# Memory-augmented attention and linear attention interleaved: row transposes moved to DMA, shared weight loads, merged left scores, column tiles throughout, a new instruction order

## The chip, the cores and the metric

The kernel runs on one core of one Trainium2 chip. Its engines run at the same time, each through a queue of its own in a fixed order: PE (TensorE, matmuls; weight loads are a queue of their own beside it, PEld), DVE (VectorE), ACT (ScalarE), POOL (GpSimd) and SP (SyncE); the last two mostly issue DMAs here. Semaphores order work between engines. The metric is the device time of one execution in microseconds. Before the change it is 1606.12 us, the median of 3 runs (1605.98 to 1608.79).

## The reference

A sequence of 2048 rows of 512 numbers (bf16) goes through four blocks with residuals: x = x + A(norm(x)), x = x + B(norm(x)), and both once more with the same weights.

```python
# A: memory-augmented attention, 32 heads of 128, segments of 32 rows, 8 memory rows
mem = mem0
for s in range(n_seg):                       # 64 segments, one after the other
    h = concat([mem, x[:, 32*s:32*s+32]])    # 40 rows
    q, k, v = h@Wq, h@Wk, h@Wv               # 512 -> 32 x 128 each
    p = softmax(mask(q k^T / sqrt(128)))
    o = (p v) @ Wo
    mem = o[:, :8]                           # feeds the next segment
    outs.append(o[:, 8:])
# B: linear attention, 32 heads of 16
q, k, v = split(x @ wqkv)
pq, pk = phi(q), phi(k)                      # phi(t) = (t+1 if t>0 else exp(t)) + 1e-6
kv, z = pk^T v, sum(pk)                      # over all 2048 rows
o = (pq kv / (pq z + 1e-6)) @ wo
```

The 8 memory rows that a segment puts out go into the next segment. So the 128 segments of both A blocks are a recurrence, and the second A block of a row tile can start only when the B block before it has seen all rows.

## The kernel before

The sequence is cut into 16 tiles of 128 rows, four segments to a tile. All weights stay in SBUF. `a_layer` runs the 64 segments of an A block. `layer` 0 is the first pair of blocks, `layer` 1 the second.

A segment's matmuls get 32 of its 40 rows as stationary operand: the 8 memory rows and 24 of the 32 new rows. The other 8 rows of each segment (the *left* or displaced rows) are put together for four segments into one block of 32 rows, which is projected once for each tile (`left_block`, steps left0, left1, leftv). A stationary operand of 32 columns fills a quarter of the array, so four matmuls with the same stationary rows run side by side in four column tiles; below, four such matmuls are a *quad*. `project` (L1140) does this for K, Q (halves b = 0 and 1 of the heads: steps kq0, kq1) and V. For several parts it loads the stationary rows for the first part (L1159) and runs the others again on them (L1055, `again`). `fresh` says for how many matmuls the later part loads anew; for V it is set from `FRESH`.

For each half of the heads, `turned` copies K and Q from PSUM and turns them by a 32x32 block transpose on DVE (L1177). `mem_attention` then makes the scores of the segment (L1260) and of the displaced keys against the memory's queries (L1266), their exponential (L1277), two mask multiplies (L1287), the sums, their reciprocal as exp(-ln) (L1296, L1298), the product with V and the normalisation (L1309): these are the rows that become the next memory. `x_attention` does the same for the other rows, later and off the recurrence. The scores of the displaced queries against the displaced keys are made once for a tile, in the step lefts (L1209) at the end of `left_block`, with their exponential (L1216) and mask (L1218).

`out_proj` multiplies by Wo (64 matmuls of 256 columns, L1402). The result stands as two halves in PSUM partitions 0 to 63 and 64 to 127, which have to be added. Two copies of 128x128 bring it to `outW` as fp32. `next_mem` (L1426) adds the halves, turns the 8 rows with a selection matrix in fp32 on PE, and a copy puts them into the next segment's block. `rows_out` adds the halves once more on DVE (L1437) for the residual, and DMAs on POOL and SP put the rows in place (dx_sb).

`layernorm` (L1093) normalises a tile of rows (L1105) and turns it by 16 transposes on PE (L1113); `prepare` (A) and `b_in` (B) copy the turned tile out of PSUM. `b_in` projects K, V and, transposed, Q, applies `phi`, and adds to the sums kva and za. In layer 0 it uses matmuls on the whole 128x128 array (`whole`, L1051), in layer 1 column tiles (`tiled`, L1067). Q is stored transposed in a DRAM scratch (pq_scratch), the rows in another (xs_scratch). `b_mid` masks the sums and folds wo in. `b_out` loads both again, divides (L1669 to L1672) and adds the product to the rows. In layer 0 it runs within the segments of the next A block; in layer 1 all 16 tiles stand at the end.

The order is written out by hand. Every operation is added under a place (layer, step, name, number), and a table gives each place a number; operations with two possible engines have a letter for ACT or DVE. `schedule` sorts all operations by this number, and each engine's queue runs in that order, so a waiting instruction holds all that stand behind it on its engine. Before the change the table is a period of four segments (`PERIOD`) with exceptions (`OWN`). `spin` adds matmuls without use, at the start and between blocks.

## Time and profile before

| what | value |
|---|---|
| runs, median (lowest to highest) | 1606.12 us (1605.98 to 1608.79) |
| span of the profiled execution, first to last instruction | 1603.9 us |
| PE busy | 1542.4 us, 96% |
| weight loads busy | 881.7 us, 55% |
| DVE busy | 1219.1 us, 76% |
| ACT busy | 1101.0 us, 69% |
| POOL busy | 200.1 us, 12% |
| DMA, mean over the span | 32 GB/s |
| weights land (Wk, Wq, Wv after issue) | 13.8, 24.5, 34.0 us |

The profile shows one execution; its span is the time from the first to the last instruction, and the time of a run lies a little above it. An engine's busy time counts moments in which at least one of its instructions runs. Matmuls overlap, so the busy time of a group of them says nothing of what it adds to the stream; the distance between the start of one and the start of the next does. "Idle before, releaser" names what an engine waited for. The chain goes back from the last instruction to what released it, step by step. A few matmul records are missing from the trace.

### The profile page before, as it was taken

The page shows a single profiled execution, that of the slowest core. Times are in us where ns is not written, and L with a number is a line of the kernel's source. Part 1 is how long each engine was busy: PE and PEld are TensorE (multiplying, and loading weights), DVE is VectorE, ACT ScalarE, POOL GpSimd, SP SyncE. Part 2 cuts the span into 40 slices and gives each one's busy share as a digit, 9 for nine tenths or more (in the row PEclk, how much of TensorE's full clock was granted, in tenths as well). Part 3 has the DMA queues.
Part 4 walks back from the last instruction along what each step waited for, and adds up shares of the span by engine and source line. Part 5 has one row for each costly group of instructions (what it writes and reads, how often), then busy time and mean ns, then how long its engine had stood idle before and what let it go on. Part 6 is the DMA issues. An engine that isn't in the chain of part 4 may idle for free.

```text
span 1603.9 us, 104195 instructions
## 1 busy us (share of the span) xinstructions
PE 1542.4 (96%) x52074; PEld 881.7 (55%) x43287; DVE 1219.1 (76%) x3865; ACT 1101.0 (69%) x3212; POOL 200.1 (12%) x408
## 2 busy tenths in 40 slices
PE   5899999999999999999999999999999999999997
PEld 1455555556555555555545565655655556556564
DVE  3778788877888887887677777777777777777777
ACT  1566666766666677676566777777778777777765
POOL 2011110111111111111101111111110111110110
PEclk9999999999999999999999999999999999999999
DMA  9300000000000000000000000000000000000014
GB/s 380 106 13 14 10 17 16 17 17 14 17 10 18 16 17 17 18 16 16 26 8 14 17 17 20 20 14 17 20 18 19 20 14 17 21 18 18 27 34 141
DMA packets 33567, 50.95 MB, mean 32 GB/s; under 512 B 10600, under 2 KB 27272, under 8 KB 31592
## 3 DMA queue, kind: packets, MB, share of 16 engines
q1 hardware_dynamic: 19288, 26.46, 4.7%
q0 software_dynamic: 13680, 17.69, 3.7%
q8 instruction: 374, 6.13, 1.6%
q14 instruction: 65, 0.53, 0.1%
q10 hardware_dynamic: 160, 0.14, 0.0%
HBM read 29.63 MB, written 10.49 MB: 25 GB/s over the span
## 4 chain that ended last, share of the span: by engine, by line
PE 89%; DVE 4%; ACT 3%; DMA 2%; issue 1%; POOL 0%; DVEq 0%; SPq 0%
PE pb L1159 27%; PE pb L1055 23%; PE pb L1402 18%; PE pb L1067 11%; PE pb L1051 3%; DMA Wv_sb<-in_A_Wv_dram 2%; ACT arena_sb L939 2%; PE pb L1260 1%; PE pb L1426 1%; PE pb L1113 1%; PE pb L1340 1%; DVE st_sb L1099 1%; DVE arena_sb L1287 0%; DVE arena_sb L940 0%; PE pb L1209 0%
## 5 line engine op out<-in xcount | busy, mean ns | idle before, releaser
L939 ACT ACTIVATE arena_sb<-pb 128x512 bf16<-128x512 f32 (+5 forms) x1234 | 556.3, 485 | 276.3 <-PE pb L1055 181.6
L1159 PE MATMUL pb<-Wk_sb,arena_sb 128*32 128x512 bf16 x4096 | 410.7, 380 | 5.5 <-DMA Wq_sb<-in_A_Wq_dram 3.2
L1055 PE MATMUL pb<-Wq_sb,arena_sb 128*32 128x512 bf16 x4096 | 410.2, 379 | 0.0
L940 DVE CAST arena_sb<-pb 128x512 bf16<-128x512 f32 (+3 forms) x510 | 275.6, 544 | 105.7 <-PE pb L1055 66.5
L1402 PE MATMUL pb<-Wo_sb,arena_sb 128*32 128x256 bf16 x10368 | 346.7, 273 | 5.5 <-issue 2.7
L1067 PE MATMUL pb<-arena_sb 128*32 128x128 bf16 (+2 forms) x12528 | 327.2, 216 | 5.2 <-DVE arena_sb L1606 2.0
L1067 PEld LDWEIGHTS pb<-arena_sb 128*32 128x32 bf16 x12528 | 227.7, 96 | 131.0 <-issue 38.8
L1177 DVE STREAM_TRANSPOSE arena_sb<-arena_sb 128x256 f32<-128x256 f32 x640 | 261.4, 431 | 50.1 <-ACT arena_sb L939 43.5
L1159 PE MATMUL pb<-Wv_sb,arena_sb 128*32 128x512 bf16 x3136 | 281.2, 378 | 1.3 <-DMA Wv_sb<-in_A_Wv_dram 0.6
L1402 PEld LDWEIGHTS pb<-Wo_sb,arena_sb 128*32 128x32 bf16 x10368 | 258.8, 96 | 37.2 <-issue 11.3
L1159 PEld LDWEIGHTS pb<-Wk_sb,arena_sb 128*32 128x32 bf16 x4096 | 122.2, 96 | 251.7 <-issue 176.5
L955 POOL DMA_DIRECT2D dx_sb<-y_sb x252 | 128.1, 512 | 1010.7 <-DVE y_sb L1437 496.7
L1055 PE MATMUL pb<-Wv_sb,arena_sb 128*32 128x512 bf16 x1984 | 210.5, 378 | 0.0
L939 ACT ACTIVATE arena_sb<-arena_sb 32x256 bf16<-32x256 bf16 (+1 forms) x377 | 143.2, 380 | 14.5 <-DVE arena_sb L1347 4.6
L1159 PEld LDWEIGHTS pb<-Wv_sb,arena_sb 128*32 128x32 bf16 x3136 | 90.5, 96 | 78.7 <-issue 24.5
L939 ACT ACTIVATE outW_sb<-pb 128x128 fp32r<-128x128 f32 x294 | 67.6, 275 | 77.9 <-PE pb L1402 69.7
L1287 DVE TENSOR_TENSOR arena_sb<-arena_sb 128x128 bf16<-128x128 bf16 x504 | 91.7, 216 | 29.6 <-ACT arena_sb L1277 27.9
L1277 ACT ACTIVATE arena_sb<-pb 128x192 bf16<-128x192 f32 (+1 forms) x256 | 85.0, 333 | 41.6 <-PE pb L1260 38.4
L1309 DVE TENSOR_TENSOR arena_sb<-pb,arena_sb 128x128 bf16<-128x128 f32 x252 | 72.9, 289 | 50.3 <-PE pb L1067 25.2
L1159 PE MATMUL pb<-Wq_sb,arena_sb 128*32 128x512 bf16 x1024 | 103.4, 378 | 0.2
L1055 PE MATMUL pb<-Wk_sb,arena_sb 128*32 128x512 bf16 x1024 | 103.0, 378 | 0.0
L940 DVE COPY arena_sb<-arena_sb 32x256 bf16<-32x256 bf16 (+1 forms) x391 | 80.1, 208 | 9.1
(110 smaller groups left out, 1789.3 us busy)
## 6 DMA issues: line engine op xcount, KB each, us to landing
Wk_sb<-in_A_Wk_dram SPq DMA_DIRECT2D x1, 4096.0 KB, 13.8
Wq_sb<-in_A_Wq_dram SPq DMA_DIRECT2D x1, 4096.0 KB, 24.5
Wv_sb<-in_A_Wv_dram SPq DMA_DIRECT2D x1, 4096.0 KB, 34.0
Wo_sb<-in_A_Wo_dram SPq DMA_DIRECT2D x16, 256.0 KB, 7.3
xs_scratch<-x_sb POOLq DMA_DIRECT2D x32, 128.0 KB, 2.8
pq_scratch<-arena_sb POOLq DMA_DIRECT2D x32, 128.0 KB, 3.1
x_sb<-xs_scratch POOLq DMA_DIRECT2D x16, 128.0 KB, 2.4
arena_sb<-pq_scratch POOLq DMA_DIRECT2D x16, 128.0 KB, 2.4
```

The costliest lines, as they stand in the source:

```text
L939: return e.activation(o() if callable(o) else o, i() if callable(i) else i, ACTF.Copy)
L940: return e.tensor_copy(o() if callable(o) else o, i() if callable(i) else i)
L955: add(eng, lambda e: e.dma_start(o, i), 0.55 if eng == "pool" else 0.4, reads=reads, writes=writes, dsem="%s%d" % (kind, k), lat=lat + (0. ...
L1051: return pe.matmul(o, w, x, start=start, stop=stop, skip_group_check=True)
L1055: return pe.add_instruction(mybir.InstMatmult(name=nc.get_next_instruction_name(), engine=mybir.EngineType.PE, ins=[pe.lower_ap(x), pe.low ...
L1067: r = pe.matmul(o[q], w[:, q], x, start=start, stop=stop, skip_group_check=True, tile_position=(0, 32 * j))
L1159: r = pe.matmul(o, blk[:, c, :], w, start=(c == 0), stop=(c == 3), tile_position=(0, 32 * j))
L1177: add("dve", lambda v: v.transpose(dst, src(img[:, k, :].bitcast(F32))), 0.445, reads=[("img", k)], writes=[dkey])
L1277: add("act", lambda a: a.activation(PQ[:, r2, b, 0:nq], tl.f32()[:, 0:nq], ACTF.Exp, scale=SCALE), c_act(nq), tiles=[tl], writes=[("PQ", r ...
L1287: add("dve", lambda v, a=a, p_=p_, w_=w_: v.tensor_tensor(wide(Pm[:, k, a, :]), p_.unsqueeze(2).to_broadcast([128, 4, 4, 8]), w_, ALU.mult ...
L1309: add("dve", lambda v: v.tensor_tensor(oTb[:, s % NO, 16 * b:16 * b + 16, 0:8], pv.f32()[:, 0:128].rearrange("p (n q) -> p n q", q=8), Rm[ ...
L1402: r = pe.matmul(tl.f32()[32 * j:32 * j + 32, 0:256], oT[:, 4 * hh + n, :], Wo_sb[:, 8 * n + hh, 256 * d:256 * d + 256], start=(hh == 0 and ...
```

## The change

It has these parts:

- *Row transposes.* `layernorm` gets a destination. With one, the normalised tile goes to it by a transposing DMA on SP (`turn`), with no matmul and no PSUM copy. `prepare` uses it for all tiles but the first (into `xT`, which lies on `vtmp`), `b_in` for all but the last (into `xlnT`). The normalised tile has two buffers.
- *B block.* `b_in` runs in column tiles in both layers. K, V and Q are projected from one weight load (Q by rows, no longer transposed); the key-value product makes only the 32x32 blocks on the diagonal (kva has 128 columns instead of 512); the key sums are one row per head group, and `b_mid` turns them on PE. Q is stored by rows, and `b_out` and `last_rows` load it with transposing DMAs from SP (before, plain ones from POOL and SP).
- *Projections.* `FRESH` is 0, so V always runs again on the weights loaded. In the second half of the heads (kq1) K and Q are projected one after the other, each with its own loads.
- *Scores.* The step lefts is gone. The displaced keys' matmul in `mem_attention` now takes the memory's and the displaced queries (64 columns instead of 32). Probabilities stand in blocks of 8 queries for four heads. The exponential comes in two parts, 64 columns for the memory first and then 160; one mask multiply replaces two.
- *Output.* One copy (64x256) brings one half out of PSUM, and DVE adds the other into `y_sb` (bf16). `next_mem` and the residual both read that; the matmuls of `next_mem` are bf16.
- *Order.* The table (`PLACE`) names every operation of every step, with no period. The new order is another in all steps; among others the first segment's scores stand ahead of its V projection.

The diff, cut to its core:

```diff
-PERIOD = {
-    0: (44811, 18084, {
...
-OWN = {
...
+PLACE = {
+    (0, -2, 'left0'): '24454 24886 25965 26396 27036a 28340 28987a 29421',
...
 def when(key, engs):
...
+    t, eng = _PLACE[key[:3]][key[3]]
     return t, eng or engs[0]
...
+    def turn(o, i, reads, writes, kind, lat=3.0):
+        add("sp", lambda e: e.dma_start_transpose(o, i), 0.45, reads=reads, writes=writes, dsem=kind, lat=lat)
+
+    def layernorm(t, after=None, dst=None):
         k = ln_no[0] % 2
+        xln = xln2[:, k, :]
...
+        if dst is not None:
+            turn(dst[0], xln, [("xln", k)], dst[1], dst[2])
+            return None
...
-        FRESH = {0: 15, 1: 21}
+        FRESH = {0: 0, 1: 0}
...
-            at(step, "lefts")
-            tl = P.tile()
-            for b in range(2):
-                def mm(pe, b=b):
...
         def prepare(G, step):
...
-            tl = layernorm(G, busy)
+            tl = layernorm(G, busy, None if G == 0 else (xT, ["vtmp"], "dtx"))
...
             def left(pe):
                 for j in range(4):
-                    r = pe.matmul(tl.f32()[32 * j:32 * j + 32, 160:192].rearrange("p (i x) -> p i x", i=4),
-                                  kTl[:, g2, b, g, j // 2, j % 2::2], qT[:, hs, j // 2, 0:8, j % 2], start=True, stop=True,
-                                  tile_position=(0, 32 * j))
+                    q = qT[:, hs, j // 2, :, j % 2].rearrange("p i (k x) -> p i k x", x=8)[:, :, 0::4, :]
+                    o = tl.f32()[32 * j:32 * j + 32, 0:384].rearrange("p (k r) -> p k r", k=2)[:, :, 0:32]
+                    r = pe.matmul(o.rearrange("p k (i x) -> p i k x", i=4),
+                                  kTl[:, g2, b, g, j // 2, j % 2::2], q, start=True, stop=True, tile_position=(0, 32 * j))
...
+                add("act", lambda a: a.activation(PQ[:, r2, b, 0:64], tl.f32()[:, 0:64], ACTF.Exp, scale=SCALE), c_act(64),
+                    tiles=[tl], writes=[("PQm", r2, b)])
...
-            add("act", lambda a: a.activation(PQ[:, r2, b, 0:nq], tl.f32()[:, 0:nq], ACTF.Exp, scale=SCALE), c_act(nq),
+            add("act", lambda a: a.activation(PQ[:, r2, b, 64:224], tl.f32()[:, 64:224], ACTF.Exp, scale=SCALE), c_act(160),
                 tiles=[tl], writes=[("PQ", r2, b)])
...
-            for a, (p_, w_) in enumerate(((main_p, main_w), (left_p, left_w))):
-                add("dve", lambda v, a=a, p_=p_, w_=w_: v.tensor_tensor(
...
+            add("dve", lambda v: v.tensor_tensor(
+                Pm[:, k, :].rearrange("p (a j x) -> p a j x", a=2, j=4),
...
                     def pvx(pe, i=i, b=b, pv=pv):
...
-                        r = tiled(pe, o, vimg[:, r2, e], Pbx[:, hh, :, :], i == 0, False)
+                        m = Pbx[:, :, b, :].rearrange("p j (k i q) -> p j k i q", k=4, i=4)[:, :, :, i, :]
+                        r = tiled(pe, o, vimg[:, r2, e], m, i == 0, False)
...
-            for h in range(2):
-                cs = slice(128 * h, 128 * h + 128)
-                evac(outW[:, w, cs], lambda cs=cs: tl.f32()[:, cs], 128, tiles=[tl],
-                     writes=[("outW", w, h)])
-            return w, tl
+            k = int(w == NW - 1)
+            a, c = (slice(0, 64), slice(64, 128))[::1 if urgent else -1]
+            v = w if urgent else 0
+            evac(outW[c, v, :], lambda: tl.f32()[c, 0:256], 256, tiles=[tl], writes=[("outW", w)])
+            add("dve", lambda e: e.tensor_tensor(y_sb[0:64, k, :], tl.f32()[a, 0:256], outW[c, v, :], ALU.add),
+                c_dve(256), reads=[("outW", w)], tiles=[tl], writes=[("y", k)])
+            return k
...
-                        r = pe.matmul(tl.f32()[32 * j:32 * j + 32, 16 * h:16 * h + 16], outW[:, w, o:o + 32].bitcast(F32),
-                                      selm_sb[:, :].bitcast(F32), start=True, stop=True, tile_position=(0, 32 * j))
+                        r = pe.matmul(tl.f32()[32 * j:32 * j + 32, 16 * h:16 * h + 16], y_sb[:, 0, o:o + 32],
+                                      selm_sb[:, :], start=True, stop=True, tile_position=(0, 32 * j))
...
-                tk, tq = project(blk, bk, (Wk_sb, "Wk", b, True), (Wq_sb, "Wq", b, True))
+                parts = (Wk_sb, "Wk", b, True), (Wq_sb, "Wq", b, True)
+                if b:
+                    tk, tq = [project(blk, bk, p)[0] for p in parts]
+                else:
+                    tk, tq = project(blk, bk, *parts)
...
     def b_in(layer, step, t):
 
-        wide, mode = (whole, 1) if layer == 0 else (tiled, 0)
...
+        end = t == NT - 1
+        tl = layernorm(t, busy, None if end else (xlnT, ["xlnT"], "dtb"))
...
+                    for i, (o, dst) in enumerate(parts):
+                        for j in range(4):
+                            q = slice(32 * j, 32 * j + 32)
+                            if i:
+                                r = again(pe, dst.f32()[q, :], xlnT[:, c, q], wqkv_sb[:, c, o:o + D], c == 0, c == 3, (0, 32 * j),
+                                          True)
+                            else:
+                                r = pe.matmul(dst.f32()[q, :], xlnT[:, c, q], wqkv_sb[:, c, o:o + D], start=c == 0, stop=c == 3,
+                                              skip_group_check=True, tile_position=(0, 32 * j))
...
+            rows((D, tk), (2 * D, tv), (0, tq))
...
+                for j in range(4):
+                    o = 128 * c + 32 * j
+                    x = pe.matmul(kv.f32()[32 * j:32 * j + 32, 32 * c:32 * c + 32], vB_sb[:, o:o + 32], e_sb[:, o:o + 32],
+                                  start=True, stop=True, skip_group_check=True, tile_position=(0, 32 * j))
...
+            for j in range(4):
+                x = pe.matmul(z.f32()[32 * j:32 * j + 32, 0:128], one_sb[:, 32 * j:32 * j + 32], e_sb[:, 128 * j:128 * j + 128],
+                              start=True, stop=True, tile_position=(0, 32 * j))
...
+        phi(tq, eq_sb, "eq")
+        x_move(pq_view[t], eq_sb, t % NX, ["eq"], [("pq", t)], "dpq")
...
+        def mzt(pe):
+            for i in range(4):
+                x = pe.matmul(tz.f32()[32 * i:32 * i + 32, 0:16], za[:, 32 * i:32 * i + 32], sel4_sb[:, :], start=True, stop=True,
+                              tile_position=(0, 32 * i))
...
-            x_move(e, pq_view[t], k, [("pq", t)], ek, "dql" if t else "dq0")
+            turn(e, pq_view[t], [("pq", t)], ek, "dtq")
```

## The prediction

> **What bounds the kernel now.** I read the page first: busy times, slices, chain.
>
> ```profile
> span 1603.9 us, 104195 instructions
> PE 1542.4 (96%) x52074; PEld 881.7 (55%) x43287; DVE 1219.1 (76%) x3865; ACT 1101.0 (69%) x3212; POOL 200.1 (12%) x408
> PE   5899999999999999999999999999999999999997
> PEclk9999999999999999999999999999999999999999
> ...
> PE 89%; DVE 4%; ACT 3%; DMA 2%; issue 1%; POOL 0%; DVEq 0%; SPq 0%
> ```
>
> PE is busy from 50 us to the end at full granted clock, and 89% of the chain lies on it. So PE's own stream is the time, and an edit is worth what it takes out of that stream, less new waits. Next the PE groups by form: the transposes (L1113), left scores (L1209), next-memory matmuls (L1426, fp32) and whole-array matmuls (L1051, 128*128, layer 0's B block) are what the change touches.
>
> ```profile
> L1426 PE MATMUL pb<-selm_sb,outW_sb 128*32 128x16 f32 x2016 | 41.0, 185 | 2.7 <-ACT outW_sb L939 2.2 <-ACT arena_sb L939 0.2
> ...
> L1051 PE MATMUL pb<-arena_sb 128*128 128x128 bf16 x320 | 26.6, 220 | 0.5 <-issue 0.3 <-DVE arena_sb L1586 0.2
> L1113 PE MATMUL pb<-id_sb,arena_sb 128*32 128x128 bf16 x1024 | 26.5, 223 | 10.9 <-DVE arena_sb L1105 10.2 <-issue 0.4
> L1051 PE MATMUL pb<-arena_sb 128*128 128x512 bf16 x81 | 25.0, 381 | 5.4 <-issue 4.4 <-DVE arena_sb L940 0.8 <-ACT arena_sb L1277 0.2
> L1209 PE MATMUL pb<-arena_sb 128*32 128x32 bf16 x1024 | 18.0, 179 | 0.0
> ```
>
> Matmuls overlap, so their durations can't be added. I charge each from its start to the next one's start. The timeline shows how; its columns are start, length, line.
>
> ```profile
> 428.10 0.23 PE L1055 MATMUL pb<-arena_sb,one_sb 128*32 128x128 bf16 x4
> 428.27 0.62 PE L1051 MATMUL pb<-arena_sb 128*128 128x128 bf16 x8
> 428.82 0.39 PE L1067 MATMUL pb<-arena_sb 128*32 128x128 bf16 x24
> ...
> 430.85 0.41 PE L1113 MATMUL pb<-id_sb,arena_sb 128*32 128x128 bf16 x16
> 431.09 0.83 PE L1402 MATMUL pb<-Wo_sb,arena_sb 128*32 128x256 bf16 x24
> ...
> 433.53 0.29 PE L1426 MATMUL pb<-selm_sb,outW_sb 128*32 128x16 f32 x16
> 433.66 0.39 PE L1159 MATMUL pb<-Wq_sb,arena_sb 128*32 128x512 bf16 x4
> ```
>
> A transpose of one tile costs 0.24 us, the next-memory step 0.13, and eight whole-array matmuls 0.55 plus a gap of about 0.1 ahead of them. A "quad" (four column-tile matmuls side by side) costs 0.2155 us at 512 columns, 0.055 at 128 and about 0.03 at 32.
>
> Then the period: in the timeline the next-memory step starts at 129.59 and, 52 segments on, at 735.37: 46.6 us per four segments in layer 0. From 864.60 to 1482.45 it is 47.5 in layer 1. The table by stretches (us, PE busy, then the other engines) leaves PE idle for 0.5 us of a layer-0 period (6.7 in 13) and 0.8 of a layer-1 period:
>
> ```profile
> 129.59:735.37 605.78, 599.05 (x19919) 340.96 (x16413) 491.19 (x1571) 415.44 (x1247) 74.63 (x144) 1.00 0.06 16
> 864.60:1482.45 617.85, 607.05 (x21629) 359.55 (x18162) 463.00 (x1497) 468.01 (x1368) 79.45 (x152) 1.00 0.07 18
> ```
>
> Last, the recurrence alone: the first segments have little other work, and there the steps follow at 10.66 and 10.47 us:
>
> ```profile
> 61.20 0.42 PE L1426 MATMUL pb<-selm_sb,outW_sb 128*32 128x16 f32 x16 [0.38 <-ACT outW_sb L939]
> ...
> 71.86 0.42 PE L1426 MATMUL pb<-selm_sb,outW_sb 128*32 128x16 f32 x16 [0.28 <-ACT outW_sb L939]
> ...
> 82.33 0.42 PE L1426 MATMUL pb<-selm_sb,outW_sb 128*32 128x16 f32 x16 [0.41 <-ACT outW_sb L939]
> ```
>
> **The change part by part**, per period of four segments, 16 periods in each layer.
>
> *B block of layer 0.* Its whole-array matmuls cost 3.1 us by start times. Three kinds of matmul that both layers run alike (L1402, and L1055 with ones and block ones) take 1.05 us more in layer 0, where they stand beside mode changes; part of this is records that are missing (81 of 128 passes are there). Together 4.15. New: K, V and Q under one load, 12 quads of 512 (2.59), four of 32 (0.12), one of 128 (0.06): 2.77. Gain 1.4. Layer 1 is in column tiles already: only narrower key-value products and sums go, gain 0.15.
>
> *Row transposes* (prepare and b_in, all but the first or last tile): 32 matmuls a period, 0.45 us, gain 0.43. PSUM copies of the turned tile go too (0.42 us on DVE or 0.60 on ACT), off the path.
>
> *Left scores*: L1209 goes, gain 0.23; its exponential and mask (0.38 ACT, 0.29 DVE) were beside PE. The merged matmul has 64 columns instead of 32, on eight quads: 0 to 0.4 us (a 32-column quad takes 0.03, a 64-column one between 0.03 and 0.08 with the gap behind it). I take 0, since 64 columns stream in a quarter of the 0.107 us of 256.
>
> *Next memory* in bf16: 0.61 now, 0.22 by the layer-1 row of 16 eight-column matmuls (0.11), gain 0.39.
>
> *Weight loads.* 576 fresh Wv loads go (L1159 has 3136 of them, and 2560 are needed); keys and queries of the second half no longer share loads, which adds 16 in each of 128 segments, 2048 or 512 quads. Rows: keys loaded fresh (L1159) take 6.92 us per 128 in layer 1, queries without load (L1055) 6.90. The loads hide; cost 0, and if nothing hid them 512 x 0.096 = 49 us.
> The Trainium skill speaks against this edit: "TensorE: Matmul & The Clock Gate", Part 3, lets a weight load overlap running matmuls only where the row group differs, and column tiles share theirs. By that rule the sum would be 49 us worse; the two rows above contradict it.
>
> *Other reads.* Probabilities are now read in runs of 8 elements. The scores' matmul already reads every second element (L1260) at the floor, so 0.
>
> Stream gain: layer 0 1.4 + 0.43 + 0.23 + 0.39 = 2.45, layer 1 0.15 + 0.43 + 0.23 + 0.39 = 1.2. Times 16: 39 + 19 = 58 us.
>
> *Wait for the turned tile.* It replaces a PE step by a DMA on SP, queued among the row moves (dx). In b_in the new table puts 2.3 to 4.9 us of PE work, 2.9 at the median by this trace's costs, between the normalisation's place and the first K matmul. The normalisation takes 0.41 on DVE; the transfer is not in this trace. Nearest rows: 128 KB to DRAM 2.8 to 3.1 us, from DRAM 2.4; below, 12 KB take 1.9; above, 512 KB take 4.5 to 6.0. I take 3.0, the same bytes. 0.41 + 3.0 - 2.9 = 0.5 us wait, 30 times: 15 us given back (0 at 2.4 us or less; 105 at 6.0). Everything behind the K matmul on PE, the next projections too, waits with it. In prepare 3.3 us or more stand in between: 0. The 16 loads in b_out move from POOL to SP and have other tiles' work ahead: 0.
> The Trainium skill, "Advanced Engine Details and Errata", X-Bar Transpose, says that transposing DMAs are as fast as plain ones; with the 2.4 of a plain load the sum would be 15 us better. No run here shows one yet.
>
> *The recurrence's chain.* Added: the sum of both halves (L1437, 0.42 us with its handover nearer 0.5) now stands ahead of the next memory, after one copy of 64x256 instead of two of 128x128 (0.28 each). Removed: one of two mask multiplies (0.22), part of the exponential (0.33 for 192 columns; 64 come first now, and 96 columns take 0.25), and keys are ready four quads (0.86) earlier in the second half. About even: 0; bounds -6 us (PE's 14 waits of 0.6 for the mask multiply L1287 in that stretch of layer 1 shrink by 0.3, times 16/13) and, where all is exposed, the rival below.
>
> *Head.* The first out projection starts at 46.03, pauses, goes on at 48.20; the scores now come ahead of V. 0 to 4 us, I take 2. *Middle and end.* The z product through PE adds about 0.5 us twice, the narrower kva sum takes 0.4 off. Four transposing loads of up to 512 KB are issued near 1557 to 1565 and first used at 1578: 12 us of cover against 4.5 today; without it, what they are late.
>
> Sum: -58 + 15 - 2 = -45. The profiled span 1603.9 becomes 1559. The median of the runs lies 2.2 us above the span (1606.1), so **1561 us**.
>
> **The rivals.** *The turned tiles come late: slower.* Each us beyond 3.0 costs 30 us in b_in; 45 are eaten at 4.5 us, the landing of a 512 KB load. At 6.0 us it is 30 x 3.0 = 90 us over mine, 1651. For it: 80 such transfers, none seen in this trace, on a queue that also waits for row moves. Against: the same bytes land in 2.4 to 3.1. Chance 0.14.
> *The recurrence becomes the bound.* Layer 0's period would be 46.6 - 2.45 + 0.5 = 44.65, 11.2 us a segment, against 10.5 for the bare chain. If the added sum lengthens it by 0.5 net and it meets uneven filler, 0.3 us is lost in each of 126 segments: 38 us, 1599. For it: little slack. Against: the three cuts above. Chance 0.11.
> *The added loads are not hidden:* with nine tenths of their 49 us exposed the gain is gone, 1561 + 45 = 1606. Chance 0.03.
> *Waits shrink too:* no wait for the tile (15), 6 us off the mask multiply, the head's full 4: 1538 and below. Chance 0.04.
>
> **How the numbers follow.** My forecast, 1543 to 1582, has 0.68. Within 0.2% (3 us) is what a measurement can't tell from no change. Faster: 0.68 + 0.11 + 0.04 = 0.83; same 0.03; slower 0.14. The range 1536 to 1602 takes in the forecast, the recurrence case and most of the last, leaving out about 0.18.
>
> **What would show it.** No L1051-like 128*128 group in layer 0, PE matmul count down, periods near 44.7 and 46.8 (47.5 - 1.2 + 15 waits of 0.5 over 16 periods); waits of PE's K matmuls in b_in for a DMA of about 0.5 us, 30 times; fresh Q quads at 0.2155. I am wrong if the transposing DMAs land above 4 us, if the next-memory step waits for the sum in every segment, or if key and query quads grow.

## The result and the profile after

The kernel became slower, where I had forecast that it gets faster. The median is 1643.88 us (1642.91 to 1649.09, 4 runs) against 1606.68 us before (1605.98 to 1608.79, 4 runs). The ratio is 1.0231, 95% interval 1.0212 to 1.025. The forecast was 1561 us (1536 to 1602). The profiled execution is the longest of the four, 5.2 us above the median, so what follows from its trace may be too large by that much. One run of e6 below, 1969.71 us at a granted clock of 0.754, is left out of its median.

The page of the changed kernel, with its busy times, slices, DMA packets and chain:

```profile
span 1647.0 us, 97785 instructions
PE 1544.7 (94%) x48837; PEld 820.7 (50%) x40483; DVE 1219.7 (74%) x3603; ACT 1056.1 (64%) x3097; POOL 191.5 (12%) x388
PE   5799999999999998999899999999999999999987
PEclk9999999999999999999999999999999999999998
...
DMA packets 79892, 58.28 MB, mean 35 GB/s; under 512 B 59416, under 2 KB 74168, under 8 KB 77944
...
q8 instruction: 351, 5.75, 1.5%
...
PE 73%; DVE 10%; DMA 8%; ACT 5%; issue 3%; SPq 1%; POOL 0%; DVEq 0%; POOLq 0%; ACTq 0%
```

PE has 3237 matmul records fewer (48837 against 52074), and its busy time is 2.3 us *longer*. PE's part of the chain fell from 89% to 73%; DVE's rose from 4% to 10%, DMA's from 2% to 8%. So the path no longer runs down PE alone. The same groups of instructions as before, by form (busy time, mean ns, then PE's idle time ahead of them and what ended it):

```profile
L2345 PE MATMUL pb<-Wo_sb,arena_sb 128*32 128x256 bf16 x10368 | 341.5, 273 | 12.4 <-issue 8.6 <-DMA Wo_sb<-in_A_Wo_dram 1.6 <-ACT arena_sb L1893 0.7
...
L2512 PE MATMUL pb<-arena_sb 128*32 128x512 bf16 x528 | 53.5, 379 | 10.1 <-DMA arena_sb<-arena_sb 8.2 <-DVE arena_sb L1894 1.1 <-ACT outW_sb L1893 0.5
L2217 PE MATMUL pb<-arena_sb 128*32 128x64 bf16 x1024 | 53.2, 194 | 2.9 <-DVE arena_sb L2139 2.5
...
L2371 PE MATMUL pb<-selm_sb,y_sb 128*32 128x16 bf16 x1008 | 28.6, 174 | 7.5 <-DVE y_sb L2354 6.3 <-issue 0.5
```

The whole-array group and the left scores are gone. The merged scores (L2217) and the bf16 next-memory step (L2371) stand in their places, and PE now waits for the sum (L2354) and for the turned tile (the `<-DMA` of L2512, the K matmuls of `b_in`).

The table by stretches, over the same 52 segments in each layer (from the first operand: start and end, length, then PE's busy time):

```profile
140.88:754.58 613.70, 594.32 (x19152) 322.52 (x15844) 473.28 (x1413) 413.61 (x1242) 73.95 (x142) 1.00 0.09 20
883.60:1514.53 630.93, 606.20 (x19563) 327.48 (x16239) 484.50 (x1441) 428.44 (x1257) 72.92 (x140) 1.00 0.11 23
```

A period of four segments is now 47.21 us in layer 0 and 48.53 in layer 1 (before 46.60 and 47.53; forecast 44.7 and 46.8). In 13 periods PE stands idle for 19.4 and 24.7 us, where it was 6.7 and 10.8.

Idle time alone doesn't tell how much the stream shrank, so I charged start to start again: from each matmul group's start to the next one's, less the usual (median) slot of its kind, with every excess over 50 ns counted as a wait.

| per period, us | layer 0 before | layer 0 after | layer 1 before | layer 1 after |
|---|---|---|---|---|
| whole | 46.60 | 47.21 | 47.53 | 48.53 |
| stream without waits | 46.4 | 43.87 | 45.91 | 44.90 |
| waits | 0.2 | 3.34 | 1.62 | 3.63 |

(For layer 0 before, about 27 of 29.7 us in 13 periods lie at the mode changes (from column tiles to the whole array and back), where records are missing too, and count as stream, as in the prediction.) The stream shrank by 2.5 and 1.0 us a period, 56 us in 32 periods. The waits grew by 3.1 and 2.0, which is 82 us. The whole span divides as follows, by the first, the 63rd, the 64th and the last of the 126 next-memory steps (the head is what comes ahead of the first, the tail what comes behind the last); experiments below are in the table too:

| profiled execution | head | layer 0, 62 segments | between | layer 1 | tail |
|---|---|---|---|---|---|
| before | 50.9 | 719.2 | 47.6 | 734.9 | 51.3 |
| after | 59.9 | 728.8 | 48.7 | 749.0 | 60.6 |
| e3, next memory off the sum | 59.6 | 723.7 | 47.4 | 741.6 | 60.4 |
| e4, tail loads later | 59.2 | 725.6 | 48.3 | 747.3 | 54.7 |
| e6, before with B tiles | 51.9 | 736.1 | 48.5 | 735.4 | 51.8 |
| e7, before with bf16 next memory | 49.6 | 721.2 | 47.7 | 749.7 | 52.2 |
| e8, before with both | 50.7 | 739.7 | 47.1 | 748.9 | 51.4 |
| e9, before with more loads | 49.1 | 739.1 | 48.2 | 764.4 | 51.8 |
| e15, before with fewer loads | 50.7 | 731.9 | 48.0 | 759.3 | 51.6 |
| e11, three edits, order as written | 54.2 | 721.4 | 47.3 | 746.8 | 53.9 |
| e14, three edits and four row buffers, order sorted anew | 50.8 | 714.0 | 46.6 | 736.4 | 49.8 |

So after against before: head +9.0, layer 0 +9.6, layer 1 +14.1, tail +9.3, between +1.1; together 43.1, the difference of the two spans (by the medians it is 37.2).

**Head.** The timeline of the changed kernel (start, length, instruction):

```profile
42.40 2.77 SPq L2049 DMA_TRANSPOSE arena_sb<-arena_sb  x1
...
52.40 0.29 DVE L1894 COPY arena_sb<-arena_sb 128x128 bf16<-128x128 bf16 x2 [6.90 <-DMA arena_sb<-arena_sb]
...
52.65 0.62 PE L2121 MATMUL pb<-Wq_sb,arena_sb 128*32 128x512 bf16 x4 [4.05 <-DVE arena_sb L1894]
...
53.47 0.64 PE L2121 MATMUL pb<-Wq_sb,arena_sb 128*32 128x512 bf16 x4
53.90 0.64 PE L2010 MATMUL pb<-Wk_sb,arena_sb 128*32 128x512 bf16 x4
```

Tile 1's normalised rows are turned by a DMA that SP issues at 42.40, directly behind the weight loads it has been issuing, and they land at 52.4: 10 us, while the median of these transfers is 3.3. DVE stands 6.9 us before them and PE 4.05. Afterwards the quads start 0.43 us apart instead of 0.2155: the granted clock (the number behind the engines' busy times) is 0.66 over 50 to 60 us, where it was 0.92 before, and 1.00 again from 60 us. After the change, then before:

```profile
50.00:60.00 10.00, 7.35 (x92) 1.59 (x52) 2.71 (x9) 1.91 (x5) 0.00 (x0) 0.66 0.14 17
...
50.00:60.00 10.00, 9.56 (x326) 5.14 (x266) 4.75 (x15) 6.10 (x20) 0.77 (x1) 0.92 0.21 64
```

The Trainium skill has this in "TensorE: Matmul & The Clock Gate", Part 1: an idle window throttles PE to half rate. Here the trace agrees, with PE's 4.05 us of idle time ahead of the slow quads.

**Tail.** The timeline where layer 1's last tile ends:

```profile
1590.82 2.11 SPq L2614 DMA_TRANSPOSE Wq_sb<-pq_scratch  x1
...
1595.31 7.39 SPq L2614 DMA_TRANSPOSE Wq_sb<-pq_scratch  x3
1602.74 2.10 SPq L1909 DMA_DIRECT2D dx_sb<-y_sb  x3
1606.10 0.42 DVE L2354 TENSOR_TENSOR y_sb<-pb,outW_sb 64x256 bf16<-64x256 f32 x1 [8.50 <-DMA dx_sb<-y_sb]
1606.58 0.62 PE L2022 MATMUL pb<-y_sb,selz_sb 128*32 128x256 bf16 x8 [6.44 <-DVE y_sb L2354]
```

Four transposing loads hold SP for 1.6 to 3.8 us each, 9.4 us together. Three row moves (dx) stand behind them and go out at 1602.74, so the last sum waits 8.50 us on DVE and PE 6.44.

### The profile page after: what moved, and what is told of

Read it like the earlier page. It is cut to its first block, busy times and chain, and to the rows that moved or that the text cites. A ratio compares the mean times of both kernels' runs of the same rounds, so it can differ in the third digit from the quotient of the medians.

```text
span 1647.0 us, 97785 instructions
## 1 busy us (share of the span) xinstructions
PE 1544.7 (94%) x48837; PEld 820.7 (50%) x40483; DVE 1219.7 (74%) x3603; ACT 1056.1 (64%) x3097; POOL 191.5 (12%) x388
## 2 busy tenths in 40 slices
DMA packets 79892, 58.28 MB, mean 35 GB/s; under 512 B 59416, under 2 KB 74168, under 8 KB 77944
## 4 chain that ended last, share of the span: by engine, by line
PE 73%; DVE 10%; DMA 8%; ACT 5%; issue 3%; SPq 1%; POOL 0%; DVEq 0%; POOLq 0%; ACTq 0%
PE pb L2121 26%; PE pb L2010 19%; PE pb L2345 14%; PE pb L2022 8%; DMA arena_sb<-arena_sb 3%; DVE arena_sb L1894 2%; ACT arena_sb L1893 2%; DMA dx_sb<-y_sb 2%; PE pb L2512 2%; DMA Wq_sb<-in_A_Wq_dram 1%; PE pb L2209 1%; DVE arena_sb L2139 1%; DVE st_sb L2058 1%; PE pb L2371 1%; DVE y_sb L2354 1%
## 5 line engine op out<-in xcount | busy, mean ns | idle before, releaser
L1893 ACT ACTIVATE arena_sb<-pb 128x512 bf16<-128x512 f32 (+3 forms) x1039 | 503.8, 511 | 300.9 <-PE pb L2010 154.7
L1894 DVE CAST arena_sb<-pb 128x512 bf16<-128x512 f32 (+3 forms) x600 | 316.9, 535 | 93.0 <-PE pb L2010 47.0
L2121 PE MATMUL pb<-Wk_sb,arena_sb 128*32 128x512 bf16 x4096 | 368.5, 381 | 5.0 <-DMA Wk_sb<-in_A_Wk_dram 2.1
L2022 PE MATMUL pb<-arena_sb 128*32 128x128 bf16 (+2 forms) x10800 | 264.0, 208 | 13.1 <-DVE arena_sb L1894 5.1
L2022 PEld LDWEIGHTS pb<-arena_sb 128*32 128x32 bf16 x10800 | 183.9, 95 | 136.1 <-DVE arena_sb L1894 36.9
L1893 ACT ACTIVATE arena_sb<-arena_sb 32x256 bf16<-32x256 bf16 (+2 forms) x396 | 141.2, 359 | 45.9 <-DVE arena_sb L2293 30.1
L2121 PEld LDWEIGHTS pb<-Wq_sb,arena_sb 128*32 128x32 bf16 x3072 | 86.4, 97 | 117.9 <-issue 50.3
L1894 DVE COPY arena_sb<-arena_sb 32x256 bf16<-32x256 bf16 (+2 forms) x522 | 103.1, 201 | 23.5 <-DMA arena_sb<-arena_sb 12.8
L2354 DVE TENSOR_TENSOR y_sb<-pb,outW_sb 64x256 bf16<-64x256 f32 x162 | 67.8, 419 | 65.0 <-ACT outW_sb L1893 52.7
L2257 DVE TENSOR_TENSOR arena_sb<-pb,arena_sb 128x128 bf16<-128x128 f32 x252 | 73.1, 290 | 54.2 <-ACT arena_sb L2245 22.4
L2010 PE MATMUL pb<-Wk_sb,arena_sb 128*32 128x512 bf16 x1024 | 104.1, 384 | 0.4 <-issue 0.4
L1893 ACT ACTIVATE outW_sb<-pb 64x256 f32<-64x256 f32 x134 | 50.6, 377 | 82.5 <-PE pb L2345 78.8
```

The lines of the kernel that those rows point to most:

```text
L1893: return e.activation(o() if callable(o) else o, i() if callable(i) else i, ACTF.Copy)
L1894: return e.tensor_copy(o() if callable(o) else o, i() if callable(i) else i)
L2010: return pe.add_instruction(mybir.InstMatmult(name=nc.get_next_instruction_name(), engine=mybir.EngineType.PE, ins=[pe.lower_ap(x), pe.low ...
L2022: r = pe.matmul(o[q], w[:, q], x, start=start, stop=stop, skip_group_check=True, tile_position=(0, 32 * j))
L2121: r = pe.matmul(o, blk[:, c, :], w, start=(c == 0), stop=(c == 3), tile_position=(0, 32 * j))
L2257: add("dve", lambda v: v.tensor_tensor(oTb[:, s % NO, 16 * b:16 * b + 16, 0:8].rearrange("p (i j) q -> p j i q", i=4), heads(pv.f32()[:, 0 ...
```

## The experiments

Experiments e1 to e5 and e10 to e14 start from the changed kernel, e6 to e9 and e15 from the one before. Every ratio is against runs of the kernel before on the same chip (medians 1606.5 to 1610.0).

**e1: the tiles of `b_in` turned on PE again.** My first suspect was the term that I had priced highest, the wait for the turned tile.

```diff
+        pe = TURN.get(P.place)                 # the 30 b_in steps
-        if dst is not None:
+        if dst is not None and pe is None:
             turn(dst[0], xln, [("xln", k)], dst[1], dst[2])
             return None
+        ... 16 transposes on PE, one copy out of PSUM
```

> The changed kernel, 1643.9 us, with the 30 tiles of the B block's input turned by PE again (16 matmuls of 0.24 us and one PSUM copy of 0.42 to 0.60 us each), the prepare tiles still by DMA, all other places in the order kept. Theory D (turned tiles that come by DMA hold the in-order queues of PE, DVE and ACT): PE's own work grows by 30 x 0.24 = 7 us, the 8.2 us of PE's waits for that transfer and about as much again behind DVE's and ACT's waits go, so 1632 to 1640. Theory R (the recurrence's chain, which now holds the sum of both halves, has become the bound): nothing comes back, 1644 to 1651.

Measured: 1651.92 us (1648.03 to 1653.04), ratio 1.0275 (1.0259 to 1.0292), 8 us *slower* than the changed kernel. PE's waits of 8.2 us for the transfer go, and 30 times 0.24, or 7 us, of transposes are back on PE. So this trade brings nothing: the time is above both expectations. Since edits in an order that was not made for them can cost by themselves (e6 to e15), it doesn't show that the wait is free.

**e2: the tiles of `prepare` turned on PE again**, by the same edit for the other 30 tiles.

> The changed kernel with the 30 tiles of the row preparation turned by PE again, each copied from PSUM once into the same buffer, the B block's tiles still by DMA. Theory D: the first transfer, which the trace has from 42.4 to 52.4 us behind the weight loads, no longer stalls the head (9 us), the later ones no longer hold DVE and ACT (some 10 us of waits, of which perhaps half reach PE), and 7 us of PE work come back: 1632 to 1640, and the first next-memory step near 52 instead of 59.9 us. Theory R: only the head comes back, less 7 us: 1641 to 1645.

Measured: 1652.95 us (1646.96 to 1655.85), ratio 1.0281 (1.026 to 1.0302). The head fell from 59.9 to 54.4 us, as the timeline above suggests, and the two layers gave it back (730.9 and 753.4 us against 728.8 and 749.0). So turning the first tile on PE is worth 5 us, and turning the other 29 there, in this order, is worth less than nothing. The time is above both expectations.

**e3: the next memory taken off the sum.** One copy of 128 partitions in bf16; the selection matmul adds the halves again, as before the change, and the sum on DVE serves only the row moves.

```diff
-    outW = sb("outW_sb", [128, NW - 1, 256], F32)
+    outW = sb("outW_sb", [128, NW, 256])
...
-            evac(outW[c, v, :], lambda: tl.f32()[c, 0:256], 256, tiles=[tl], writes=[("outW", w)])
+            evac(outW[n, w, :], lambda: tl.f32()[n, 0:256], 256, tiles=[tl], writes=[("outW", w)])
...
-                        r = pe.matmul(tl.f32()[32 * j:32 * j + 32, 16 * h:16 * h + 16], y_sb[:, 0, o:o + 32],
+                        r = pe.matmul(tl.f32()[32 * j:32 * j + 32, 16 * h:16 * h + 16], outW[:, w, o:o + 32],
```

> The changed kernel with the next memory taken from the copy of the out projection (all 128 partitions in bf16, a selection that adds the two halves in PE) and no longer from DVE's sum y, which stays for the row moves alone; same order, no instruction more in the segments. Theory R: each of 126 segments has its memory 0.4 to 0.5 us earlier where it is waited for; PE's waits for y ahead of the next memory (6.3 us) and what stands behind them go: 1615 to 1630. Theory D: the chain is covered by other work in most segments: 1638 to 1643.

Measured: 1635.78 us (1634.55 to 1636.99), ratio 1.0181 (1.0167 to 1.0195), 8.1 us less, between the two expectations. The step's row, by form, before and after the edit (that of the changed kernel, with 6.3 us behind L2354, is shown above):

```profile
L2380 PE MATMUL pb<-selm_sb,outW_sb 128*32 128x16 bf16 x1008 | 29.9, 171 | 0.5 <-issue 0.4
```

The idle time ahead of the step fell from 7.5 to 0.5 us. The sum's place on the recurrence did cost, about as much as PE's waits for it say.

**e4: the tail's transposing loads behind the last row moves** (a number in the order, nothing else).

```diff
+                P.forced = None if w else (1520301 + i, "sp")
```

> The changed kernel with the four transposing loads of the final output stage issued on SP behind the last row moves instead of among them. In the trace of the changed kernel SP spends 9.5 us on issuing them between 1590.8 and 1602.7, the row moves wait behind, DVE's sum waits 8.5 us for a row move and PE 6.4 us for that sum. Theory D (queue): the wait goes and the first use at 1618 still has some 8 us: 1636 to 1639. Rival (the loads are then late for their own use): 1642 to 1646.

Measured: 1638.3 us (1637.29 to 1640.65), ratio 1.0199 (1.0184 to 1.0213), 5.6 us less; the tail went from 60.6 to 54.7. On SP the row moves now stand ahead (timeline of SP):

```profile
1580.46 12.02 SPq L1915 DMA_DIRECT2D dx_sb<-y_sb  x5
...
1592.52 9.64 SPq L2621 DMA_TRANSPOSE Wq_sb<-pq_scratch  x4
1602.20 2.33 SPq L2620 DMA_DIRECT2D Wq_sb<-xs_scratch  x4
```

The four loads still hold SP for 9.64 us. No wait of PE or DVE in the tail ends with a DMA now.

**e5: every K, Q and V matmul with its own weight load** (4096 loads more than the changed kernel).

```diff
-                    tk, tq = project(blk, bk, *parts)
+                    tk, tq = project(blk, bk, *parts, fresh=16)
...
-... fresh=(FRESH[layer] + g) // 4)):
+... fresh=16)):
```

> The changed kernel with a weight load for every key, query and value matmul of the segments (kq0's queries and the second V half take a load of their own instead of sharing one): 4096 loads or 1024 quads more, nothing else changed. If loads hide behind the running quads, as the prediction took from the layer-1 rows: 1643 to 1647. If they don't (the rule of the Trainium skill that the prediction weighed): 1024 x 0.096 = 98 us more, 1742.

Measured: 1643.37 us (1641.42 to 1650.55), ratio 1.0237 (1.0215 to 1.0259): no change. The page shows the loads (44579 against 40483) beside an unmoved PE:

```profile
PE 1545.4 (94%) x48837; PEld 911.7 (56%) x44579; DVE 1220.6 (74%) x3603; ACT 1057.8 (64%) x3097; POOL 192.5 (12%) x388
```

They take 91 us more of PEld's time and none of PE's. The rule of the Trainium skill weighed in the prediction ("TensorE: Matmul & The Clock Gate", Part 3) would have added 1024 times 0.096, or 98 us, here; this run contradicts it for quads of 512 columns.

**e6, e7, e8: parts of the change put into the kernel before, its order untouched.** If PE's stream were the time, each would be faster by the prediction's prices. e6 puts layer 0's B block into column tiles, e7 makes the next-memory step bf16, e8 does both.

```diff
-        wide, mode = (whole, 1) if layer == 0 else (tiled, 0)
+        wide, mode = tiled, 0
```

```diff
-    selm_sb = sb("selm_sb", [128, 16], F32R)
+    selm_sb = sb("selm_sb", [128, 16])
...
-    outW = sb("outW_sb", [128, NW, 256], F32R)
+    outW = sb("outW_sb", [128, NW, 256])
```

> The kernel before, 1606, with one edit: layer 0's B block in column tiles as layer 1 has it, the order kept. By the prediction's sum (PE's own stream is the time) the block costs 4.15 us by start times today and about 2.9 in column tiles with the wider key-value product: 16 x 1.25 = 20 us less, 1584 to 1590. If the shorter stream only turns into waits, as in the changed kernel: 1600 to 1606.

> The kernel before with one edit: the copy of the out projection, the selection and so the next-memory matmuls in bf16 (16 passes less a segment, 0.39 us of PE's stream a period by the prediction), order kept. By the prediction's sum 32 x 0.39 = 12 us less: 1592 to 1596. If it turns into waits: 1602 to 1606.

> The kernel before with both edits, column tiles in layer 0 and the bf16 next memory, in its own order. By the prediction's sum 20 + 12 us: 1574 to 1582. If the shortened stream meets the recurrence's chain or the queues of DVE and ACT: more than the two single runs' gains added up, 1585 to 1600.

Measured: e6 1627.41 us, ratio 1.014 (1.0119 to 1.016); e7 1622.63, ratio 1.0097 (1.0083 to 1.011); e8 1639.39, ratio 1.0207 (1.0191 to 1.0223). By the prediction's prices each shortens PE's stream, and each is slower, by 20, 15 and 32 us, more than either expectation had; e8's is less than the two together (35). (Column tiles need more instructions: e6 has 1536 weight loads more and as many matmuls; e7 has 1008 of each fewer, e8 528 more.) In the table e6 loses 17 us in layer 0, which it edits, and nothing in layer 1. e7 loses 2 in layer 0 and 15 in layer 1, though it makes the same edit in both. PE's list of waits in e8 shows the new kind of wait; "issue" is time in which the profile names nothing that PE waited for:

```profile
PE pb L1067 <- issue: 15.0, 28, 1.4
PE pb L1402 <- issue: 13.4, 15, 1.4
PE pb L1067 <- DVE arena_sb L1287: 12.1, 27, 0.8
```

In the kernel before, the same two lines stood at 2.4 and 2.7 us (`<- issue`), and the wait for the mask multiply L1287 was much as here, 11.4. What PE waits for at "issue" can be seen in one of them. The timeline of e8:

```profile
294.21 0.60 PE L1402 MATMUL pb<-Wo_sb,arena_sb 128*32 128x256 bf16 x13
296.12 0.53 PE L1402 MATMUL pb<-Wo_sb,arena_sb 128*32 128x256 bf16 x11 [1.32 <-issue]
```

and its DMA view from 292 to 296.5 us, in 40 slices of 0.11 us:

```profile
DMA  0000000000000000050000000000000000000000
...
DMA packets 1, 0.02 MB, mean 4 GB/s; under 512 B 0, under 2 KB 0, under 8 KB 0
...
q8 instruction: 1, 0.02, 1.3%
```

PE stops in the midst of one step, between two matmuls with the same kind of operands, for 1.32 us. The only transfer about is one packet of 16 KB on the instruction queue, near 293.9; PE goes on 2 us later. PE's instructions come in such packets, 256 at a time: the trace's PE instructions divided by these packets give 255.9 to 256.5 in every kernel here. I took every stall of PE over 0.4 us with no releaser and asked whether it ends 1.2 to 2.0 us behind the end of such a packet: 57 of 62 do in e8, 37 of 37 in e7, 38 of 40 in e6, 24 of 28 in the changed kernel, 13 of 23 in the kernel before. By chance it would be one in five.

Their place says more. Number all of PE's instructions, weight loads included, by their starts, from 0. In the six kernels e6, e7, e8, e14, e15 and the changed one, every stall with no releaser that puts the next start over 0.4 us beyond the usual distance (233 in all) falls on a number that leaves 193 or 194 when divided by 256: always at the step from one packet's instructions to the next's. The 256 instructions ahead of such a stall ran in 2.8 to 3.1 us at the median, those ahead of steps without one in 4.1 to 4.5. So PE stands there for its next instructions, mostly behind dense stretches.

The stalls sum as follows, with the bound at 0.15 us and 1.15 to 2.2 us behind a packet, beside what the layer lost in the table:

| kernel | layer 0: stalls, us | lost against before | layer 1: stalls, us | lost against before |
|---|---|---|---|---|
| before | 13.7 (mostly mode changes) | | 2.7 | |
| e6 | 28.9 | 16.9 | 2.6 | 0.5 |
| e7 | 8.4 | 2.0 | 20.1 | 14.8 |
| e8 | 40.5 | 20.5 | 19.1 | 14.0 |
| after | 7.9 | 9.6 | 14.4 | 14.1 |

(What of before's 13.7 falls in that distance behind a packet is chance: the mode changes come at all times.) In e6 the stalls rise in the layer that loses, in e7 in the one that loses, in e8 in both. In the changed kernel they account for layer 1 in size and not for layer 0, where no rise is seen.

**e9 and e15: weight loads added to the kernel before, and taken away.** If PE stalls where its instructions come too late, more loads (each is an instruction) should cost and fewer should not.

```diff
-                tk, tq = project(blk, bk, (Wk_sb, "Wk", b, True), (Wq_sb, "Wq", b, True))
+                tk, tq = project(blk, bk, (Wk_sb, "Wk", b, True), (Wq_sb, "Wq", b, True), fresh=16)
...
-... fresh=(FRESH[layer] + g) // 4)):
+... fresh=16)):
```

(e15 has only the last line, with `fresh=0`.)

> The kernel before, 1606, with a weight load of its own for every key, query and value matmul of the segments: 5568 loads more, nothing else changed, in its own order. PE's instructions come in packets of 256, and in the traces 24 of the changed kernel's 28 longest stalls without a releaser (57 of 62 in the kernel before with both edits) end 1.2 to 2.0 us behind such a packet, where chance would give a fifth. Theory I (instruction supply: a denser instruction stream stalls PE until the next packet is there): 22 packets more in the busiest stretches, stalls up by 15 to 40 us, 1618 to 1645, while the quads themselves keep their 0.2155 us. Theory H (loads hide and cost nothing, as in the changed kernel where 4096 more made no difference): 1604 to 1610. By the rule of the Trainium skill that the prediction weighed, 1392 quads x 0.096 = 134 us: 1740.

> The kernel before, 1606, with the 576 weight loads of its V projection left out that repeat a load already made: PE's instructions fall by 2.25 packets, nothing else changes. If the old kernel is simply bound by its instruction supply, 22 packets more cost 41 us, so 2 packets fewer give 4 us: 1601 to 1604. If its order is fitted to its durations, so that any change of PE's rhythm costs: 1608 to 1620.

Measured: e9, with 5568 loads more, 1649.4 us (1645.23 to 1654.91), ratio 1.0259 (1.0239 to 1.0278), 41 us slower, a little above what the theory of late instructions expected. The quads themselves still start 0.2155 us apart; what grew are waits at "issue":

```profile
PE pb L1067 <- issue: 10.3, 13, 2.3
PE pb L1402 <- issue: 9.6, 20, 0.8
PE pb L1159 <- issue: 6.6, 12, 1.2
```

e15, with 576 loads *fewer*, is slower too: 1644.01 us (1641.35 to 1650.98), ratio 1.0217 (1.0195 to 1.0239), 34 us, far above both expectations. Its "issue" waits are of the same kind:

```profile
PE pb L1067 <- issue: 10.6, 17, 1.2
...
PE pb L1402 <- issue: 6.8, 17, 1.0
PE pb L1426 <- issue: 4.2, 7, 0.8
```

In layer 1 the stalls behind packets rose from 2.7 us to 30.3 in e9 and 26.2 in e15, about what that layer lost (29.5 and 24.4). In layer 0 (22.3 and 14.3, losses 19.9 and 12.7) before's mode changes hide what is new. So the amount of instructions isn't what decides: e5 adds 4096 to the changed kernel for nothing, and e15 takes 576 away and pays 34 us. What the five edits share is that the order of before was kept while something in it changed. All five also change the number of PE's instructions, and with it which of them stand at a step between two packets; none keeps that number, so they don't tell an order fitted to durations from one that happens to lie well to the packets. In the kernel before, six of the 13 periods of layer 0 in the table by stretches take 46.37 us and the others 46.04 to 47.72. In the changed kernel they scatter between 45.70 and 51.36.

**e10: the changed kernel's instructions in an order sorted anew**, with a search over the order that uses durations from the traces; some 1100 copies change between ACT and DVE, and no instruction is added or removed.

```diff
+RANK = _split("""
+10 13 11 12 19 20 22 23 28 29 30 32 35 36 37 38 76 100 119 140 173 174 21 1
...
```

> The changed kernel's own instructions, all of them and no other, in a new order: each engine's queue locally re-sorted (a place moves by 2 to 3 instructions on average) and 1100 of the copies moved between ACT and DVE, for the durations, handovers, transfer landings and their scatter that the traces of the changed kernel show, instead of the fixed costs of the written table. Theory O (the instructions are cheaper as predicted, but the written order fits durations and landings that are too short, and each miss becomes a PE wait): 1605 to 1625. Theory C (the dependency chain and the added sum themselves are longer; no order helps): 1636 to 1644.

Measured: 1636.19 us (1633.38 to 1639.47), ratio 1.0178 (1.0163 to 1.0193), 7.7 us less: by the traces it gains in the head, the tail and layer 1 (53.8, 57.6 and 743.2 us) and not in layer 0 (728.9). That is in the range of theory C, at its lower edge, and not in that of theory O: a new order alone doesn't mend the changed kernel.

**e11 and e12: e3, e4 and tile 1 turned on PE, together;** e11 in the order as written, e12 sorted anew.

> The changed kernel in its written order with three edits together: the next memory taken off the sum, the transposing loads of the end behind the row moves, and tile 1's preparation turned by PE alone. From the single runs (8, 6 and 5 us where they act): 1622 to 1628 if they add up, up to 1636 if they overlap.

> The kernel of the run before this one (three edits) with its order re-sorted in the same way as the changed kernel's. Theory O: the gains add up, 1585 to 1605, faster than the kernel before. Theory C: like the run before it, 1620 to 1630.

Measured: e11 1624.28 us (1623.02 to 1631.64), ratio 1.0111 (1.0093 to 1.0128), 19.6 us less than the changed kernel: the single gains (8.1, 5.6 and the head's 5.5) add up. e12 1610.62 (1605.16 to 1617.37, 12 runs), ratio 1.0024 (1.0009 to 1.0038): the order is worth 14 more, short of theory O's range and far from theory C's.

**e13 and e14: four buffers for rows instead of three.** DVE's waits for loads between 100 and 1545 us had grown from 0.9 us to 18; the longest are for rows of x.

```diff
-    NX = 3
+    NX = 4
```

> The three edits in the written order (1624.3 us) with four row buffers instead of three, so that the load of a tile's rows no longer waits for the store of the tile three before it. Theory B (row loads hold DVE's queue: 9 us of DVE waits for them in layer 0 of the changed kernel): 1614 to 1619. Theory S (supply and order): 1622 to 1626.

> The kernel of the run before this one with its order re-sorted like that of the run at 1610.6 us, now with the wait for PE's instruction packets counted among the costs. Theory S: 1598 to 1607, PE's waits without a releaser below those of the run at 1610.6. Theory B alone: 1605 to 1610, since the order was re-sorted there too.

Measured: e13, the order as written, 1623.35 us (1620.41 to 1624.25), ratio 1.0078 (1.0062 to 1.0094), against e11's 1.0111 in other runs: at best 5 us, and the medians differ by 1. Waits for rows aren't what still separates e11 from before. e14, sorted anew for the four buffers, with a charge for late instructions, is 1604.17 us (1599.43 to 1608.83, 11 runs), ratio **0.996 (0.9948 to 0.9972)**. This is faster than both kernels, by 0.4% against before. Its page:

```profile
span 1597.6 us, 97857 instructions
PE 1517.1 (95%) x48853; PEld 838.5 (52%) x40499; DVE 1199.1 (75%) x3533; ACT 1067.7 (67%) x3168; POOL 192.4 (12%) x390
```

In this execution, the shortest of the 11, PE is busy for 25 us less than before, but idle for 80.5 us of the span where it was idle for 61.5. The time is in theory S's range but not for its reason: the stalls at the steps between packets sum to some 30 us in the two layers, as in e12.

## Why the prediction was wrong

**"So PE's own stream is the time, and an edit is worth what it takes out of that stream, less new waits."** This is the step that failed, in its second half. The stream shrank as worked out: 2.5 us a period against 2.45 in layer 0, 1.0 against 1.2 in layer 1, 56 us against 58. The bf16 next-memory step gave less than the 0.39 us a period that I took: its mean, from its start to the next matmul's, fell from 0.152 to 0.087 us in layer 0 and from 0.147 to 0.125 in layer 1, so 0.26 and 0.09 in four steps.

But I priced new waits only where the diff names a new dependency, at 15 us. The runs show 82 us of waits more in the two layers. In the 26 periods of the table, 91 us of waits stand after the change: 22.5 end with the sum or the turned tile, 28.5 have no releaser (20.9 of them at a step between packets), and 40 end with other results of DVE and ACT. Before, the last kind had 24, and off the mode changes some 3 had no releaser. So two thirds of the new waits stand at no dependency that the diff adds, and the largest share of them is late instructions. That little idle time before (6.7 us in 13 periods) belongs to the work only together with its order: e6, e7, e8, e9 and e15 leave the order of before as it was, three of them with a shorter stream by the prediction's prices and one with fewer loads, and all are 15 to 41 us slower. That the matmul count and the PE share speak for a PE bound was read rightly; what an edit is worth depends on its order as well. Of the 37 us, three faults that the diff adds (tile 1's transfer, the tail's loads, the sum) make up 19.6 in the written order (e11), and a new order then gives 14 (e12). Even the fastest kernel here, e14, stays some 40 us above the forecast, so no order tried here turned most of the shorter stream into time.

**Wait for the turned tile, 15 us.** The landing was near: 3.0 us taken, 3.3 the median. The rows of the DMA issues, after the change and, for the last, before it:

```profile
arena_sb<-arena_sb SPq DMA_TRANSPOSE x60, 3.3
arena_sb<-pq_scratch SPq DMA_TRANSPOSE x16, 3.3
x_sb<-in_A_x_dram POOLq DMA_DIRECT2D x15, 128.0 KB, 3.3
...
arena_sb<-pq_scratch POOLq DMA_DIRECT2D x16, 128.0 KB, 2.4
```

The first 3.3 is of the 30 transfers in `b_in`, whose landing the trace has: 2.4 to 5.2 us, nine of them above the 4 us that I had named as a sign of being wrong. That transposing DMAs are as fast as plain ones is the sentence of the Trainium skill weighed there ("Advanced Engine Details and Errata", X-Bar Transpose). The trace agrees if they are set against the plain loads of x, 3.3; but the load of Q took 2.4 as a plain one, on POOL's queue, and 3.3 as a transposing one, on SP's. PE's waits for the turned tile are 8.2 us in 8 places, not 15 in 30. Taking the transfers out of `b_in` (e1) gains nothing. So the term was mis-sized by some 7 us on the safe side, and the rival *the turned tiles come late* falls: that the time came near its 1651 was luck, for its waits in `b_in` are a tenth of its 90 us.

**"In prepare 3.3 us or more stand in between: 0", and the head's "I take 2" (a gain).** Nothing speaks against it for 29 tiles (e2 gains nothing by turning them on PE), and it is wrong for the first. I looked at the distance to the tile's use and not at what stands ahead of the transfer on SP: it is issued behind the weight loads and lands 10 us later. The head lost 9 us; 5.5 of them go with that tile (e2; in e11, where it alone is turned on PE, the head is 54.2 too).

**"Middle and end": 12 us of cover.** I asked when the four loads are first used, not who queues behind them. The four transposing loads hold SP for 1.6 to 3.8 us each; as plain loads, before the change, they held it for 0.4 to 0.6. The tail cost 9.3 us, and moving the loads gives 5.6 (e4).

**"About even: 0" for the recurrence's chain.** Wrong by 8 us: e3 gains 8.1 by taking the sum off the chain. The rival *the recurrence becomes the bound* had the mechanism and 38 us for it. It was seen at about a fifth of that size: PE waits for the sum ahead of only 13 steps of 126 (2.6 us at the longest), and at the others something else stood in between.

**Weight loads, 0.** Right: e5. The loads hide behind quads, also 4096 more of them. That each is also one of PE's instructions, and so moves the steps between packets (e9, e15), I hadn't weighed. **Merged scores with 64 columns, 0, and the strided reads, 0.** From a group of merged scores to the next matmul's start it is 0.030 us at the median, where the 32 columns took 0.028. Nothing in the traces speaks against the strided reads; they weren't tried by themselves.

What stays open: of the 24 us that the two layers lost by the traces, e3 explains 8 to 14; e14's new order brings the layers to 714.0 and 736.4 us, 3.7 below before in sum, in an execution 4.7 us under its median, and I can't divide that rest between late instructions and hand-overs from DVE and ACT. Between 62 and 1600 us, PE's waits for other engines' results, charged start to start, sum to 48 us before, 94 after, 92 in e3, 73 in e12, 68 in e14. The stalls behind instruction packets are no smaller in e14 (17.0 and 13.8 us by layer) than in the changed kernel, so what the new order recovered are waits for results; what the packets cost, no order tried here took away. Whether an order could is open.

## What to carry to other kernels

Where every queue runs in an order written out, time taken off the busiest engine can be worth nothing, or less, in the old order, as in e6, e7 and e8; judge such an edit together with an order made for it. An edit that takes away a wait can pay in the old order too (e3, e4, e11). When a DMA moves to another queue, look at both sides of it there: what stands ahead of it when it is issued (the head's 10 us) and what stands behind it while it is issued (the tail's 8.5 us). Keep additions off a recurrence even where another operation seems to leave it at the same time, and read waits at "issue" as a cost of their own beside the waits for results.

## What the runs showed of the hardware that was not expected

PE's instructions arrive during the run, in 16 KB packets of 256 instructions on a queue of their own (351 in the changed kernel, room for 89856; the records of its matmuls and weight loads are 89320). PE can run dry: stalls, mostly of 0.4 to 1.7 us, that end 1.2 to 2.0 us behind such a packet, 57 of 62 such stalls in e8, and some 40 us of them in one layer of e8. In the six kernels counted above, all those over 0.4 us without a releaser stand at the step from one 256 to the next. Adding 5568 weight loads to the kernel before costs 41 us although each quad keeps its 0.2155 us, while 4096 added to the changed kernel cost nothing; so the amount isn't what decides. The place of the stalls shows that PE waits there for its next instructions; that the density of the 256 ahead decides it (2.8 to 3.1 us against 4.1 to 4.5) is read from the traces and was not tried by itself.

A transposing DMA of 128 KB lands in 3.3 us at the median, where the medians of plain ones of that size on POOL's queue are 2.0 to 3.9, but SP, which issues it, is held for 1.2 us at the median, and for 1.6 to 3.8 us by each of the four of 384 and 512 KB; as plain loads, before the change, those held it for 0.4 to 0.6 us. The packets of the kernel rose from 33567 to 79892, those under 512 bytes from 10600 to 59416.
